# First laps of a fused attention and two-layer FFN kernel: a wider k product, weight conversions placed one to a lap, another order in the first lap

## The chip, the cores and the metric

The kernel runs on one NeuronCore of a Trainium2 chip. The metric is the device time of one execution in microseconds (us). Before the change the median of three runs is 961.79 us (961.52 to 962.55). About 0.2%, or 1.9 us, is the smallest difference that a comparison of this kernel can tell from none.

## The reference

Inputs are float32 except that the FFN weights come as float64 and stay so in DRAM; the kernel narrows them itself. Linear attention over 4 batches of 8 heads, 576 tokens, head size 64, is followed by two feed-forward layers on 2304 tokens of 512 features.

```python
def phi(x):
    proj = einsum('bhsd,df->bhsf', x, w_phi)               # 64 -> 128 features
    proj = proj - max(abs(proj), axis=-1, keepdims=True)
    return concatenate([exp(proj), exp(-proj)], axis=-1)
q_p, k_p = phi(q), phi(k)
kv  = einsum('bhsf,bhsd->bhfd', k_p, v);  z = sum(k_p, axis=2)
num = einsum('bhsf,bhfd->bhsd', q_p, kv)
den = einsum('bhsf,bhf->bhs', q_p, z)[..., None] + 1e-06
x   = (num / den), heads side by side                      # 2304 x 512
h   = x @ w_in;   x = max(0.01 h, h) @ w_out               # layer 1
h   = x @ w_in2;  out = (h * sigmoid(h)) @ w_out2          # layer 2
```

## The kernel before

Work on attention goes by pairs of heads, 16 pairs. Pairs 0 to 7 (`NFULL = 8`) are computed in full float32 in a first stage, the head; pairs 8 to 15 come later, in another form, between the matmuls of layer 1. Layer 1 goes over five tiles of about 460 tokens; for each tile it walks 16 blocks of 128 hidden features, with `emit_h(t, c)` (first product) and `emit_y(t, c)` (second). Layer 2 follows with a Strassen-like scheme.

The FFN weights must be converted from float64 before use. One conversion of a 128x512 block has a load into a tile of a ring of three (`raw`, L549), two ScalarE instructions (`ca`, L557 and L558), four VectorE instructions (`cd`, L564 to L567), a ScalarE copy to the high half (`ch`, L646) and a VectorE subtraction for the low half (`cs`, L651, recorded as L143). The conversions listed in `CONV` (L513) run in the head; the others are given to `prep` (L657) through `TODO` (L908) ahead of the blocks of the first tile.

One pair of the head takes these steps: load (`flq`, `flv`); k product on TensorE (`fpk` L290, and `fkt` for the last 64 tokens); row maximum and subtraction on VectorE (`fkd0..2`, L171 and L172); two exponentials on ScalarE (`fke`); q product (`fpq`) and its copy from PSUM on ScalarE (`fpc`, L339 and L341); the maximum over partitions on GpSimd (`fpr`, L350); its subtraction on VectorE (`fms`, L358); exponentials (`fqx`, L368 and L369); k times v on TensorE (`fkv`, L261 and L266); its copy on ScalarE (`fkc`, L378); numerator and denominator on TensorE (`fn0`, `fn1`, L391 and L395); the division on VectorE (`fnd`, L407 to L409); transposition (`fnt`) and the split into the x tiles (`ffx`, L287 and L143). A name like `fms1.0` means step `fms1` of pair 0.

The tiles `p`, `m` and `qh` have two buffers each, so the second half of one pair and the first half of the next share them in turn. PSUM banks come from a ring of eight (`bank`, L63).

The order is written out by hand. Each step of each pair has a due time: `LAP = 11.5` per pair plus an offset, with special offsets for pairs 0 to 2 in `FIRST` (L489). Each conversion has a lap and an offset kind in `LAPS` (L514). All steps are sorted by due time, and in the head `in_order` (L72) binds TensorE, ScalarE and VectorE to exactly that order. DMA issues and GpSimd are not bound. Steps due after `T0`, and everything of the FFN layers, are ordered by the planner of the framework.

```python
    for n, (lap, late) in enumerate(LAPS):
        for n_, o in (dict(cl=-14.0, ca=3.15, ...), dict(cl=-9.0, ca=1.4, ...))[late].items():
            seq.append((BASE + LAP * lap + o, n, n_))
```

So before the change laps 1, 3 and 5 hold two conversions each and laps 2 and 4 one: eight in all.

Of the kernel before, what the change touches and what calls it, by code (L numbers as in the profile page):

```python
# [19 lines left out]
def tile_linear_attention_ffn_ffn(ctx: ExitStack, tc: tile.TileContext, q, k, v, w_phi, w_in1, w_out1, w_in2, w_out2, out):  # L20


    nc = tc.nc
    B, H, S, D = 4, 8, 576, 64
    F = (w_phi.shape[1] - 128) // 3
# [9 lines left out]
    NFULL = 8  # L35
# [16 lines left out]
    def at(shape, dt, tag):  # L52
        return att_pool[0].tile(shape, dt, tag=tag, bufs=AB[0].get(tag, 1), name=tag)
# [4 lines left out]

    PRO = [True]

    ring = [0]

    def bank():  # L63

        if not PRO[0]:
            return ps("a")
        ring[0] += 1
        return ps("ay"[(ring[0] - 1) // 4 % 2])
# [16 lines left out]
    wc = at([128, 3 * F + 128], F32, "wc")  # L85
# [56 lines left out]
    def sub(out_, x, h):  # L142
        nc.vector.tensor_tensor(out_, x, h.bitcast(F32), op=ALU.subtract)  # L143

    def full(i):
        return i < NFULL
# [107 lines left out]
    def kv_sign(i, s):  # L254
        st = P[i]
        ke, va = st["ke"], st["va"]
        if s == 1:
            st["kv"] = bank()
        pv = st["kv"][:, 0 : 4 * NKV].rearrange("p (s j d) -> p s j d", s=2, j=2)
        vf = va.rearrange("p c d -> p (c d)")  # L260
        nc.tensor.matmul(pv[:, s, :, 0 : D + 1], ke[:, 8, s, :], va[:, 8:10], start=True, stop=False, skip_group_check=True)  # L261
        for j in range(2):
            for c in range(4):
                w = (4 * j + c) * (D + 1)
                g = 4 * j + c if full(i) else 2 * c + j
                nc.tensor.matmul(  # L266
                    pv[:, s, j], ke[:, g, s, :], vf[:, w : w + NKV], start=False, stop=(j == 1 and c == 3), skip_group_check=True
                )
        return pv

    def s_kv(i):
        st = P[i]
        for s in (1, 0):
            pv = kv_sign(i, s)
        h, l = st["KVH"], st["KVL"] = at([128, 2, 2, 2, D], F32R, "KVH"), at([128, 2, 2, 2, D], F32R, "KVL")
        for j in range(2):
            kv_, z_ = pv[:, :, j, 0:D], pv[:, :, j, D : D + 1].to_broadcast([128, 2, D])
            for slot, sr in ((j, kv_), (1 - j, z_)):
                nc.scalar.activation(h[:, j, :, slot, :], sr, AF.Copy)
                sub(l[:, j, :, slot, :], sr, h[:, j, :, slot, :])  # L280
# [9 lines left out]
    def f_pk(i):  # L290

        st = P[i]
        st["pk"] = [bank(), bank()]
        for c in range(4):
            for j in range(2):
                r = slice(64 * j, 64 * j + 64)
                o = st["pk"][j][:, c * F : (c + 1) * F]
                nc.tensor.matmul(o, st["kr"][r, c * 128 : (c + 1) * 128], wraw[r], start=True, stop=True)
# [159 lines left out]
    def s_fin(a):  # L458
# [13 lines left out]
    )  # L472
    head = dict(
        flq=load_qk, flv=load_v, fpk=f_pk, fkt=f_kt, fkv1=lambda i: kv_sign(i, 1), fkv0=lambda i: kv_sign(i, 0), fkc=f_kc,
        fkd0=f_kd(0), fkd1=f_kd(1), fkd2=f_kd(2), fke0=f_ke(0), fke1=f_ke(1),
    )
    for a in range(2):
        for n_, f in dict(fpq=f_pq, fpc=f_pc, fpr=f_pr, fms=f_ms, fqx=f_qx, fn=f_n, fnd=f_nd, fnt=f_nt, ffx=f_fx).items():
# [4 lines left out]
        flq=-8.0, fpq0=5.1, fpq1=5.11, fpk=6.2, fkt=7.2, fpc0=5.6, fpc1=6.2, fpr0=10.55,  # L483
# [4 lines left out]
    KEYS = {n_: o + LAP * lag for lag, d in enumerate((AHEAD, NEXT, HERE, PAST)) for n_, o in d.items()}  # L488
    FIRST = {  # L489
        0: dict(flq=-9.0, flv=-8.9, fpk=-5.0, fkt=-4.0, fpq0=-3.5, fpq1=-3.4, fpc0=-2.7, fpr0=-2.6, fke0=-2.0, fpc1=-1.0, fpr1=-0.9, fkd0=-3.4, fkd1=-2.2, fkd2=-1.0,  # L490
                fke1=-0.2, fms0=0.1, fqx0=1.7, fms1=3.3, fqx1=4.0, fn0=5.0, fn1=6.9, fnd0=7.0, fnd1=9.2),
        1: dict(flq=-8.8, flv=-8.0, fpk=-2.0, fkt=-1.0, fpq0=-0.6, fpq1=-0.5, fpc0=1.0, fpc1=2.8, fpr0=2.9, fms0=5.3, fqx0=7.0, fpr1=4.1, fms1=8.0),
        2: dict(flq=-8.5, fpq0=9.1, fpq1=9.11, fpk=10.2, fkt=11.2, fpc0=9.7, fpc1=10.3),
    }
    BASE = 8.9
# [14 lines left out]
    seq = [(T0 + LATER[i][n_] if n_ in LATER.get(i, ()) else t, i, n_) for t, i, n_ in seq]  # L510
    TL = T0 + 21.15 - min(OFF1.values())
    seq += [(TL + W * (i - NFULL) + o, i, n_) for i in range(NFULL, B * HP) for n_, o in OFF1.items()]
    CONV = [("wi", 0), ("wi", 1), ("wi", 2), ("wi", 3), ("wo", 0), ("wi", 4), ("wo", 1), ("wi", 5)]  # L513
    LAPS = [(1, 0), (1, 1), (2, 0), (3, 0), (3, 1), (4, 0), (5, 0), (5, 1)]  # L514
    for n, (lap, late) in enumerate(LAPS):
        for n_, o in (dict(cl=-14.0, ca=3.15, cd=6.1, ch=8.3, cs=10.1), dict(cl=-9.0, ca=1.4, cd=8.0, ch=8.8, cs=10.7))[late].items():
            seq.append((BASE + LAP * lap + o, n, n_))
    seq.sort()
    seq.reverse()
# [25 lines left out]
    wi, wo = {}, {}  # L545
# [39 lines left out]
    def load_wi(layer, c):  # L585
        w = (w_in1, w_in2)[layer].bitcast(U32)
        return load64(w[c].rearrange("p (f t) -> p f t", t=2))

    def load_wo64(w, c):
        return load64(w.bitcast(U32)[c * 128 : (c + 1) * 128, :].rearrange("p (f t) -> p f t", t=2))  # L590
# [28 lines left out]

    C = [dict() for _ in CONV]  # L620

    def c_load(n):

        kind, c = CONV[n]
        C[n]["raw"] = load_wi(0, c) if kind == "wi" else load_wo64(w_out1, c)
# [9 lines left out]
    def halves(kind, c):  # L635

        if kind == "wi":
            wi[0, c] = [wp.tile([128, KD, 128], F32R, tag=g, bufs=NC, name=g) for g in ("wih", "wil")]
            return [x.rearrange("p k f -> p (k f)") for x in wi[0, c]]
        wo[c] = wp.tile([128, 2, DM], F32R, tag="wo1", bufs=WOB, name="wo1")  # L640
        return wo[c][:, 0], wo[c][:, 1]

    def c_high(n):

        C[n]["h"] = halves(*CONV[n])
        nc.scalar.activation(C[n]["h"][0], C[n]["f"], AF.Copy)  # L646

    def c_low(n):

        kind, c = CONV[n]  # L650
        sub(C[n]["h"][1], C[n]["f"], C[n]["h"][0])  # L651
# [5 lines left out]
    def prep(kind, c):  # L657

        if (kind, c) in CONV:
            return  # L660
        raw = load_wi(0, c) if kind == "wi" else load_wo64(w_out1, c)
        f = narrow64(raw)
        split(f, *halves(kind, c))
        if kind == "wo":
            nc.sync.dma_start(wos[c], wo[c].bitcast(F32))
# [239 lines left out]
    split_consts()  # L905
    run_att(T0)
    PRO[0] = False
    TODO = [("wi", 6), ("wi", 7)], [("wo", 2), ("wi", 8)], [("wi", 9), ("wi", 10)], [("wo", 3), ("wi", 11)], [("wo", 4), ("wi", 12), ("wi", 13)], [("wo", 5), ("wi", 14)], [("wo", 6), ("wi", 15)]  # L908

    def jobs_of(m, p):  # L910
        for _ in prep_w7(m, p):
# [20 lines left out]
    for s, (t, c) in enumerate((t, c) for t in range(len(tiles1)) for c in range(NC)):  # L932
        if t:
            wo[c] = load_wo(c)
        else:
            for x in TODO[c] if c < len(TODO) else [("wo", c)]:
                prep(*x)
# [120 lines left out]
```

## Time and profile before

| | |
|---|---|
| median of three runs | 961.79 us |
| profiled execution, its own time | 963.05 us |
| its span | 961.3 us |
| PE busy (matmul) | 940.5 us, 98% |
| PEld busy (weight loads) | 886.3 us, 92% |
| DVE busy | 646.9 us, 67% |
| ACT busy | 596.8 us, 62% |
| POOL busy | 70.0 us, 7% |
| mean granted TensorE clock | 0.994 |

The profile is of one execution. PE is TensorE, DVE is VectorE, ACT is ScalarE, POOL is GpSimd, SP issues DMAs. Idle time of an engine is set down with what ended it. A float32 matmul is recorded as two instructions. Matmuls are pipelined and their ends are modelled, so that the start of one to the start of the next is the better measure of pace.

### The profile page before, as it was taken

What the parts mean: (1) busy time and instruction counts of PE and PEld (TensorE: products, weight loads), DVE (VectorE), ACT (ScalarE), POOL (GpSimd) and SP (SyncE); (2) the same over time, 40 slices, a digit from 0 to 9 for tenths busy, and PEclk for the clock granted to TensorE, in tenths of its full rate; (3) what the DMA queues carried; (4) which work ended last, traced back from release to release, by engine and by line L of the source; (5) the groups of instructions that cost most, each with busy time, mean ns of one, the idle gap of its engine ahead of it and who ended that gap; (6) DMA issues with size and microseconds to landing.
All of it is one profiled execution on the core that took longest, in us unless ns stands there. A gap on an engine that the chain in (4) does not pass through costs nothing.

```text
span 961.3 us, 15911 instructions
## 1 busy us (share of the span) xinstructions
PE 940.5 (98%) x5446; PEld 886.3 (92%) x5446; DVE 646.9 (67%) x1280; ACT 596.8 (62%) x1224; POOL 70.0 (7%) x38
## 2 busy tenths in 40 slices
PE   7999999999999999999999999999999999999998
PEld 6888888898999988988888999999999999999998
DVE  5899989865666655288778767777762595624853
ACT  5788877676777766466555655665554565544553
POOL 3333000211111111000000000000000000000000
PEclk9999899999999999999999999999999999999999
DMA  6443489644333332399999999896988878886884
GB/s 248 142 139 111 158 250 326 226 142 119 119 109 119 93 121 69 114 360 380 359 331 326 377 352 342 306 341 237 301 290 294 244 233 273 293 286 216 250 279 136
DMA packets 102529, 226.15 MB, mean 235 GB/s; under 512 B 15024, under 2 KB 25264, under 8 KB 102448
## 3 DMA queue, kind: packets, MB, share of 16 engines
q1 hardware_dynamic: 102160, 224.86, 70.0%
q8 instruction: 44, 0.72, 0.3%
q14 instruction: 37, 0.30, 0.1%
q10 hardware_dynamic: 288, 0.26, 0.1%
HBM read 177.82 MB, written 47.22 MB: 234 GB/s over the span
## 4 chain that ended last, share of the span: by engine, by line
PE 74%; DMA 9%; DVE 9%; ACT 5%; issue 2%; SPq 1%; POOL 0%; DVEq 0%; ACTq 0%
PE ps_y L868 18%; PE ps_y L732 15%; PE ps_a L712 14%; PE ps_a L792 10%; PE ps_y L792 8%; PE ps_a L266 3%; DMA d<-rec 2%; DMA rec<-e 2%; PE ps_a L443 1%; DVE t L566 1%; PE ps_y L391 1%; DMA qr<-in_q_dram 1%; DMA raw<-in_moe_w_in_dram 1%; PE ps_a L391 1%; DVE km L171 1%
## 5 line engine op out<-in xcount | busy, mean ns | idle before, releaser
L868 PE MATMUL ps_y<-gt,ws 128*128 128x384 f32 x1008 | 177.2, 336 | 0.0
L868 PEld LDWEIGHTS ps_y<-gt,ws 128*128 128x128 f32 x1008 | 176.5, 188 | 0.0
L732 PE MATMUL ps_y<-gh,wo 128*128 128x460 f32 (+1 forms) x640 | 150.4, 373 | 2.5 <-ACT gh L575 2.5
L732 PEld LDWEIGHTS ps_y<-gh,wo 128*128 128x128 f32 x640 | 119.0, 188 | 15.9 <-ACT gh L575 3.1
L712 PE MATMUL ps_a<-xh,wih 128*128 128x460 f32 (+1 forms) x320 | 119.5, 374 | 0.4 <-ACT g L715 0.3
L712 PE MATMUL ps_a<-xl,wih 128*128 128x460 f32 (+1 forms) x320 | 118.9, 371 | 0.0
L712 PE MATMUL ps_a<-xh,wil 128*128 128x460 f32 (+1 forms) x320 | 118.8, 371 | 0.0
L792 PE MATMUL ps_a<-xs,ws 128*128 128x384 f32 x546 | 104.7, 338 | 1.6 <-DMA ws<-w7s 1.6
L792 PEld LDWEIGHTS ps_a<-xs,ws 128*128 128x128 f32 x546 | 96.7, 188 | 2.3 <-ACT xs L575 1.9
L575 ACT ACTIVATE gt<-g 128x384 fp32r<-128x384 f32 x120 | 62.8, 524 | 52.8 <-PE ps_y L868 50.9
L143 DVE TENSOR_TENSOR gt<-g,gt 128x384 fp32r<-128x384 f32 x120 | 66.5, 556 | 35.9 <-ACT gt L575 35.5
L792 PE MATMUL ps_y<-xs,ws 128*128 128x384 f32 x462 | 88.5, 338 | 0.2 <-DVE g L768 0.2
L732 PE MATMUL ps_y<-gl,wo 128*128 128x460 f32 (+1 forms) x320 | 82.7, 373 | 0.0
L792 PEld LDWEIGHTS ps_y<-xs,ws 128*128 128x128 f32 x462 | 81.7, 188 | 0.6 <-DVE g L768 0.5
L143 DVE TENSOR_TENSOR gl<-g,gh 128x460 fp32r<-128x460 f32 (+1 forms) x80 | 50.9, 637 | 33.8 <-ACT gh L575 28.8
L715 ACT ACTIVATE g<-ps_a 128x460 f32<-128x460 f32 (+1 forms) x80 | 44.0, 551 | 38.9 <-PE ps_a L712 38.3
L712 PEld LDWEIGHTS ps_a<-xh,wih 128*128 128x128 f32 x320 | 60.1, 188 | 7.3 <-DVE ke L172 0.5
L732 PEld LDWEIGHTS ps_y<-gl,wo 128*128 128x128 f32 x320 | 60.1, 188 | 6.8
L712 PEld LDWEIGHTS ps_a<-xh,wil 128*128 128x128 f32 x320 | 60.1, 188 | 6.8
L712 PEld LDWEIGHTS ps_a<-xl,wih 128*128 128x128 f32 x320 | 60.3, 188 | 6.1
L231 POOL PARTITION_ALL_REDUCE m<-p x16 | 34.8, 2178 | 242.6 <-ACT p L229 203.7
L575 ACT ACTIVATE gh<-g 128x460 fp32r<-128x460 f32 (+1 forms) x80 | 46.7, 585 | 8.4 <-PE ps_y L732 7.4
(164 smaller groups left out, 1593.0 us busy)
## 6 DMA issues: line engine op xcount, KB each, us to landing
ws<-w7s SPq DMA_DIRECT2D x336, 256.0 KB, 3.7
wo<-wos SPq DMA_DIRECT2D x64, 512.0 KB, 4.8
w7s<-wst SPq DMA_DIRECT2D x48, 512.0 KB, 5.7
raw<-in_moe_w_in_dram SPq DMA_DIRECT2D x32, 512.0 KB, 5.1
raw<-in_moe_w_out_dram SPq DMA_DIRECT2D x32, 512.0 KB, 5.1
wos<-wo SPq DMA_DIRECT2D x16, 512.0 KB, 4.0
va<-in_v_dram SPq DMA_DIRECT2D x16, 325.0 KB, 3.4
qr<-in_q_dram SPq DMA_DIRECT2D x16, 288.0 KB, 4.2
```

The source lines that it names most:

```text
L143: nc.vector.tensor_tensor(out_, x, h.bitcast(F32), op=ALU.subtract)
L171: nc.vector.tensor_reduce(km[:, 0:ng], src, op=ALU.max, axis=AX.X, apply_absolute_value=True)
L231: nc.gpsimd.partition_all_reduce(m, p, 128, bass_isa.ReduceOp.absmax)
L266: nc.tensor.matmul(pv[:, s, j], ke[:, g, s, :], vf[:, w : w + NKV], start=False, stop=(j == 1 and c == 3), skip_group_check=True)
L391: nc.tensor.matmul(pb[:, w : w + NNUM], e[:, s, cs], KV[:, s, j], start=(s == 0), stop=(s == 1))
L443: nc.tensor.matmul(o, lhs, st[m, a][:, s, j * w : (j + 1) * w], start=(n == 0), stop=(n == 5))
L575: nc.scalar.activation(h, f, AF.Copy)
L712: nc.tensor.matmul(ph, a[:, kk, :], b_[:, kk, :], start=(m == 0), stop=(m == 3 * KD - 1))
L715: nc.scalar.activation(g, ph, AF.Prelu, alpha=0.01)
L732: nc.tensor.matmul(Y[t][d][:, 0:n], a[:, ds_], b_, start=(c == 0 and m == 0), stop=(c == NC - 1 and m == 1), skip_group_check=True)
L792: nc.tensor.matmul(bank[b_], w[:, a, kk], x[:, c, kk], start=(first and m == 0), stop=(m == 5), skip_group_check=True)
L868: nc.tensor.matmul(bank[b_][db], w[:, a, db], t[:, c], start=(first and p == 0 and m == 0), stop=(p == NP - 1 and m == 2), skip_group_chec ...
```

## The change

`fpk` of pairs 0 and 1 multiplies 128 rows by the block-diagonal weight `wc[:, 0:2F]` (256 columns, four matmuls) in place of eight matmuls of 64 rows by 128 columns. `kv_sign` reads the groups of those pairs in the matching order. In the first lap `fms1.0`, `fqx1.0` and `fkc.0` come earlier, as do `fpr0.1`, `fms0.1`, `fpr1.1` and `fms1.1`. Conversions: one in lap 0 (offset kind 2), one in lap 1 (kind 3, written as lap 0 with offsets a lap larger), one in each of laps 2, 3 and 4, two in lap 5: seven. The eighth, `("wi", 5)`, goes to the front of `TODO`.

```diff
-    ring = [0]
+    ring, WIDE = [0], 2
@@ kv_sign
-                g = 4 * j + c if full(i) else 2 * c + j
+                g = 4 * j + c if WIDE <= i < NFULL else 2 * c + j
@@ f_pk
         for c in range(4):
+            if i < WIDE:
+                o = st["pk"][c // 2][:, (c % 2) * 2 * F : (c % 2 + 1) * 2 * F]
+                nc.tensor.matmul(o, st["kr"][:, c * 128 : (c + 1) * 128], wc[:, 0 : 2 * F], start=True, stop=True)
+                continue
             for j in range(2):
@@ FIRST
-                fke1=-0.2, fms0=0.1, fqx0=1.7, fms1=3.3, fqx1=4.0, fn0=5.0, fn1=6.9, fnd0=7.0, fnd1=9.2),
-        1: dict(flq=-8.8, flv=-8.0, fpk=-2.0, fkt=-1.0, fpq0=-0.6, fpq1=-0.5, fpc0=1.0, fpc1=2.8, fpr0=2.9, fms0=5.3, fqx0=7.0, fpr1=4.1, fms1=8.0),
+                fke1=-0.2, fms0=0.1, fqx0=1.7, fms1=1.5, fqx1=2.6, fkc=2.7, fn0=5.0, fn1=6.9, fnd0=7.0, fnd1=9.2),
+        1: dict(flq=-8.8, flv=-8.0, fpk=-2.0, fkt=-1.0, fpq0=-0.6, fpq1=-0.5, fpc0=1.0, fpc1=2.8, fpr0=1.1, fms0=4.2, fqx0=7.0, fpr1=3.0, fms1=6.0),
@@ conversions
-    CONV = [("wi", 0), ("wi", 1), ("wi", 2), ("wi", 3), ("wo", 0), ("wi", 4), ("wo", 1), ("wi", 5)]
-    LAPS = [(1, 0), (1, 1), (2, 0), (3, 0), (3, 1), (4, 0), (5, 0), (5, 1)]
+    CONV = [("wi", 0), ("wi", 1), ("wi", 2), ("wi", 3), ("wo", 0), ("wi", 4), ("wo", 1)]
+    LAPS = [(0, 2), (0, 3), (2, 0), (3, 0), (4, 0), (5, 0), (5, 1)]
-        ... (dict(cl=-14.0, ca=3.15, cd=6.1, ch=8.3, cs=10.1), dict(cl=-9.0, ca=1.4, cd=8.0, ch=8.8, cs=10.7))[late]
+        ... (dict(cl=-14.0, ca=3.15, cd=6.1, ch=8.3, cs=10.1), dict(cl=-9.0, ca=1.4, cd=8.0, ch=8.8, cs=10.7), dict(cl=-7.9, ca=4.5, cd=4.6, ch=7.3, cs=15.2), dict(cl=-7.8, ca=14.65, cd=17.6, ch=19.8, cs=21.6))[late]
-    TODO = [("wi", 6), ("wi", 7)], [("wo", 2), ("wi", 8)], ...
+    TODO = [("wi", 5), ("wi", 6), ("wi", 7)], [("wo", 2), ("wi", 8)], ...
```

The order of the first lap on the three bound engines, read off the due times (steps that change place in bold):

- DVE before: fkd0.0 fkd1.0 fkd2.0 fms0.0 fkd0.1 fkd1.1 fkd2.1 fms1.0 fms0.1 fnd0.0 fms1.1 fnd1.0 fkd0.2
- DVE after: fkd0.0 fkd1.0 fkd2.0 fms0.0 fkd0.1 **fms1.0** fkd1.1 fkd2.1 fms0.1 **cd.0** **fms1.1** fnd0.0 fnd1.0 fkd0.2
- ACT before: fpc0.0 fke0.0 fpc1.0 fke1.0 fpc0.1 fqx0.0 fke0.1 fpc1.1 fqx1.0 fkc.0 fke1.1 fqx0.1 fpc0.2
- ACT after: fpc0.0 fke0.0 fpc1.0 fke1.0 fpc0.1 fqx0.0 fke0.1 **fqx1.0 fkc.0 fpc1.1 ca.0** fke1.1 fqx0.1 **ch.0** fpc0.2
- PE, both: fpk.0 fkt.0 fpq.0 fpk.1 fkt.1 fpq.1 fkv.0 fn0.0 fn1.0 fpq.2 fpk.2 fkt.2 fkv.1 fnt.0 fpq.3 fpk.3 fkt.3 fn.1 fkv.2 and so on

## Rows read from the trace of the kernel before

**Rows 1.** The page, busy tenths in 40 equal slices of the span, VectorE.
```profile
DVE  5899989865666655288778767777762595624853
```

**Rows 2.** Windows: stretch, length, then busy (count) of PE PEld DVE ACT POOL; clock, DMA, GB/s.
```profile
18.85:22.36 3.51, 3.51 (x18) 3.51 (x19) 0.00 (x0) 1.30 (x2) 1.89 (x1) 0.56 0.03 13
...
98.20:104.93 6.73, 6.73 (x37) 6.73 (x37) 6.73 (x18) 5.83 (x11) 0.00 (x0) 0.58 0.43 152
104.93:133.00 28.07, 27.25 (x174) 24.63 (x172) 25.34 (x58) 20.08 (x37) 0.00 (x0) 1.00 0.65 206
133.00:204.90 71.90, 70.26 (x362) 63.28 (x361) 60.43 (x114) 51.67 (x98) 7.03 (x3) 1.00 0.74 249
204.90:961.30 756.40, 747.99 (x4138) 712.27 (x4136) 475.93 (x929) 444.95 (x913) 27.82 (x13) 1.00 0.73 246
```

**Rows 3.** Waits of PE over the whole span: total us, times, longest.
```profile
PE ps_y L732 <- ACT gh L575: 2.5, 2, 2.3
...
PE ps_a L261 <- ACT ke L180: 1.6, 1, 1.6
```

**Rows 4.** Timeline of PE in the first lap: start us, us, instruction, [idle before <-releaser].
```profile
13.19 1.95 PE L266 MATMUL ps_y<-va,ke 128*128 128x128 f32 x16
18.85 3.52 PE L391 MATMUL ps_y<-KV,qh 128*128 128x128 f32 x16 [3.71 <-ACT KV L378]
...
25.60 1.06 PE L298 MATMUL ps_y<-wc,kr 64*128 64x128 f32 x16
...
26.91 0.39 PE L261 MATMUL ps_a<-va,ke 128*128 128x130 f32 x2
```

**Rows 5.** Timeline of PE: the end of `fn1` of pairs 0 to 4.
```profile
23.99 0.61 PE L395 MATMUL ps_a<-KV,qh 128*128 128x130 f32 x4
...
37.69 0.61 PE L395 MATMUL ps_a<-KV,qh 128*128 128x130 f32 x4
...
50.58 0.61 PE L395 MATMUL ps_y<-KV,qh 128*128 128x130 f32 x4
...
61.88 0.61 PE L395 MATMUL ps_a<-KV,qh 128*128 128x130 f32 x4
...
75.20 0.61 PE L395 MATMUL ps_y<-KV,qh 128*128 128x130 f32 x4
```

**Rows 6.** Timeline of DVE in the first lap.
```profile
9.82 1.95 DVE L358 TENSOR_TENSOR m<-p,m 128x512 f32<-128x512 f32 x1 [0.34 <-POOL m L350]
...
12.41 0.69 DVE L172 TENSOR_TENSOR ke<-ps_y,km 128x512 f32<-128x512 f32 x1
...
22.40 0.16 DVE L407 TENSOR_SCALAR d<-ps_y 128x4 f32<-128x4 f32 x1 [5.72 <-PE ps_y L391]
...
22.81 0.42 DVE L409 TENSOR_TENSOR x<-ps_y,d 128x256 f32<-128x256 f32 x1
```

**Rows 7.** Timeline of ACT in the first lap, and the start of a conversion.
```profile
16.17 0.38 ACT L339 ACTIVATE p<-ps_y 128x256 f32<-128x256 f32 x1 [1.43 <-DVE m L358]
...
16.92 0.76 ACT L368 ACTIVATE qh<-m 128x640 f32<-128x640 f32 x1
...
18.18 0.62 ACT L378 ACTIVATE KV<-ps_y 128x512 f32<-128x512 f32 x1
...
27.86 0.71 ACT L557 ACTIVATE t<-raw 128x512 f32<-128x512 f32 x1
```

**Rows 8.** Timeline of POOL: the second all-reduce of pair 0.
```profile
9.81 2.34 POOL L350 PARTITION_ALL_REDUCE m<-p  x1
```

**Rows 9.** Timeline of DVE: two conversions start in turn, and a low half.
```profile
33.48 0.42 DVE L564 TENSOR_SCALAR t<-t 128x512 f32<-128x512 f32 x1
...
35.73 0.42 DVE L564 TENSOR_SCALAR t<-t 128x512 f32<-128x512 f32 x1
...
49.85 0.69 DVE L143 TENSOR_TENSOR wil<-r,wih 128x512 fp32r<-128x512 f32 x1
```

**Rows 10.** The chain that ended last, in order of time, one piece: start, us, what.
```profile
133.52 5.48 DMA raw<-in_moe_w_in_dram
```

More of the change, by code (lines that the diff above doesn't have):

```diff
@@ L512, in tile_linear_attention_ffn_ffn @@
     seq += [(TL + W * (i - NFULL) + o, i, n_) for i in range(NFULL, B * HP) for n_, o in OFF1.items()]
-    CONV = [("wi", 0), ("wi", 1), ("wi", 2), ("wi", 3), ("wo", 0), ("wi", 4), ("wo", 1), ("wi", 5)]
-    LAPS = [(1, 0), (1, 1), (2, 0), (3, 0), (3, 1), (4, 0), (5, 0), (5, 1)]
+    CONV = [("wi", 0), ("wi", 1), ("wi", 2), ("wi", 3), ("wo", 0), ("wi", 4), ("wo", 1)]
+    LAPS = [(0, 2), (0, 3), (2, 0), (3, 0), (4, 0), (5, 0), (5, 1)]
     for n, (lap, late) in enumerate(LAPS):
-        for n_, o in (dict(cl=-14.0, ca=3.15, cd=6.1, ch=8.3, cs=10.1), dict(cl=-9.0, ca=1.4, cd=8.0, ch=8.8, cs=10.7))[late].items():
+        for n_, o in (dict(cl=-14.0, ca=3.15, cd=6.1, ch=8.3, cs=10.1), dict(cl=-9.0, ca=1.4, cd=8.0, ch=8.8, cs=10.7), dict(cl=-7.9, ca=4.5, cd=4.6, ch=7.3, cs=15.2), dict(cl=-7.8, ca=14.65, cd=17.6, ch=19.8, cs=21.6))[late].items():
             seq.append((BASE + LAP * lap + o, n, n_))
@@ L907, in tile_linear_attention_ffn_ffn @@
     PRO[0] = False
-    TODO = [("wi", 6), ("wi", 7)], [("wo", 2), ("wi", 8)], [("wi", 9), ("wi", 10)], [("wo", 3), ("wi", 11)], [("wo", 4), ("wi", 12), ("wi", 13)], [("wo", 5), ("wi", 14)], [("wo", 6), ("wi", 15)]
+    TODO = [("wi", 5), ("wi", 6), ("wi", 7)], [("wo", 2), ("wi", 8)], [("wi", 9), ("wi", 10)], [("wo", 3), ("wi", 11)], [("wo", 4), ("wi", 12), ("wi", 13)], [("wo", 5), ("wi", 14)], [("wo", 6), ("wi", 15)]
     def jobs_of(m, p):
```

## Prediction

> **What bounds the kernel now.** I read the page's slices first: TensorE shows nines almost throughout, and VectorE shows eights and nines only from the second slice to about the eighth, that is up to some 190 us, and sixes and sevens after that [rows 1]. So the changed stage lies where two engines are near full. The windows split it. From 204.90 on PE is busy for 747.99 of 756.40 us at full clock [rows 2]: whatever time is won earlier is simply carried to the end, since nothing there waits for a date. From 104.93 to 204.90 PE is busy for 97.5 of 100 us, and DVE for 85.8 [rows 2]: PE sets the pace there, but DVE is close behind, and PE's 1.6 us wait for `ke` of pair 8 [rows 3] shows that DVE's and ACT's backlog does end one thing last there. Before that, in the head, the timeline of PE shows the laps. The ends of `fn1` lie at 23.99, 37.69, 50.58, 61.88 and 75.20 [rows 5], so the laps take 13.70, 12.89, 11.30 and 13.32 us. The reader sees a pattern: 11.30 is PE's own lap, without a stall, and the longer ones follow the laps that hold two conversions, in which DVE is late. In lap 0, PE stands still for 3.71 us before `fn0.0` because ACT copies KV late, and the 16 matmuls behind that gap take 3.52 us where 16 of the same shape before it took 1.95 [rows 4]; the granted clock of that stretch is 0.56, the mean of a part at 1.2 GHz and a part at 2.4 [rows 2].
>
> **Lap 0.** Before, ACT was through with `fke0.1` at 14.74 (16.17 less its wait of 1.43), waited for DVE to free the `p` buffer, copied `fpc1.1` for 0.75 (16.92 less 16.17), did `fqx1.0` in 1.26 and reached KV at 18.18 [rows 7]. After, `fms1.0` stands right behind `fkd0.1` on DVE, which ends at 13.10 (12.41 + 0.69) [rows 6]; POOL's maximum is there at 12.15 (9.81 + 2.34) [rows 8]. At some 0.8 us it is done at 13.9, before ACT wants it. So ACT does `fqx1.0` from 14.74 to 16.0 and can copy KV then, if `fkv.0` is through. That ended at 15.14 (13.19 + 1.95) [rows 4].
>
> The wide product moves it. Its cost is not in the trace. From below: 16 instructions of the old form take 1.06 us [rows 4]; if the wide form, eight instructions, cost the same, nothing is added. From above: the same columns streamed through the whole array, 16 times 128, took 1.95 [rows 4], 0.9 more. I take 0.9, since that row streams just these columns at full clock. For pair 0 it costs nothing, since PE waits for q behind it anyway (without that cover, 0.9); for pair 1 it puts the end of `fkv.0` at 16.04, level with ACT's 16.0. KV is thus copied at 16.05, 2.1 earlier than 18.18, and `fn0.0` starts at about 16.7 in place of 18.85. PE's gap shrinks from 3.71 to about 0.7.
>
> The two halves of `fn` then take full-clock time: 3.5 us in place of 5.1 (18.85 to 23.99). The last four matmuls start at 20.3, not 23.99: 3.7 earlier. What is late next is DVE, since the conversion now stands ahead of the divisions. ACT: KV to 16.5, `fpc1.1` 0.75, two `ca` instructions of 0.71 that overlap, some 1.2 [rows 7], so `ca.0` ends at 18.45. DVE: `cd.0` 2.25 (35.73 less 33.48) [rows 9] to 20.7, `fms1.1` 0.7, `fnd0.0` 0.83 (22.40 to 23.23) [rows 6] and `fnd1.0`, half as wide again, 0.9: 23.1. `fkv.1` needs the bank that `fnd1.0` frees. PE itself had 2.92 us from `fn1.0`'s last matmuls to `fkv.1` (23.99 to 26.91) [rows 4, 5], which leads to 23.2: the two come together, and `fkv.1` starts at 23.2, not 26.91. **Lap 0 gives 3.7 us.** Its bounds: 4.2, if the steps ahead of `fms0.0` win half a microsecond too, because the wide product of pair 0 no longer waits for the second half of the weights; and a loss of 1.8, if KV comes no earlier and both wide products lie on the path at 0.9 each.
>
> The other moved steps of pair 1 (`fpr0.1`, `fpr1.1`, `fms0.1`, `fms1.1`) only follow the new order of DVE and ACT, and POOL has no other work. On SP the two raw loads of the first laps keep their place behind `flv.1`, so no load of a pair moves.
>
> On DVE, `fms0.0` took 1.95 us when it started with the all-reduce (9.82 against 9.81) [rows 6, 8], about 1.2 longer than a free one, and ended before POOL did (11.77 against 12.15). `cd.0` meets the all-reduce of `fpr1.1`, which runs from 17.3 to 19.6; its instructions with two SBUF inputs start near 19.2, past such a 1.2 us hold, so I cost this at nothing. The Trainium skill, SBUF — State Buffer, "Who interferes with whom", says that a DVE instruction with two SBUF inputs is blocked until a GpSimd instruction that reads SBUF has wholly finished. The trace disagrees on "wholly". By that rule `cd.0` would stand until 19.6 and the forecast would be some 0.5 us slower.
>
> **Laps 1 to 4.** Lap 1 was held on PE by nothing (26.91 to 37.69 is one run), so it keeps its length and the next marker falls at 34.0. Its second conversion cost the time after it: 12.89 where a lap of PE takes 11.30, a gain of 1.6. The same in lap 3: 13.32 becomes 11.30, a gain of 2.0. That one conversion fits into 11.30 is what the lap ending at 61.88 shows [rows 5]; if it does not fit four times in a row, DVE sets a lap between 11.30 and 13.32, and at worst both terms are gone. Markers: 45.3, 56.6, 67.9. **Head: 3.7 + 1.6 + 2.0 = 7.3 us earlier.** Lap 5 has two conversions before and after, and starts from PE's wait in both, so its shape should be kept.
>
> **The eighth conversion.** `wi5` now runs after the head: DVE 2.25 + 0.6 (0.69, overlapping) [rows 9], 2.9 in all, and ACT some 1.7. Its load stands ahead on SP's queue in the place that `wi6`'s had, and each later load one place later. Lower bound 0: PE is nearly gapless from 104.93 to 204.90, wi5 is read only by the sixth block of the first tile, and DVE has 2.7 us free up to 133.00 and 11.5 behind it [rows 2]. Upper bound 2.9: PE's wait for `ke` [rows 3] hangs on DVE's and ACT's order, behind the conversions, and there PE would arrive 7.3 earlier while DVE comes only 4.4 earlier. I take two thirds, 1.9, nearer to the bound since that wait exists already and the free time on DVE is partly DMA latency (a raw load took 5.48 us to land [rows 10]).
>
> **Sum.** -7.3 + 1.9 = -5.4 us. The profiled execution took 963.05 us (span 961.3), so 957.6 by its own clock; the median of the runs stands 1.26 lower, at 961.79, which gives 956.4.
>
> **Rivals.**
> - *The head's end runs better too* (chance 0.20). Behind PE's wait of 2.3 us for `gh` [rows 3], PE runs 6.73 us at clock 0.58 [rows 2]. If the planner's new order closes that gap, 6.73 x 0.42 = 2.8 us are won, and `wi5` is hidden: -10.1, 951.7. For it: PE's work is all there. Against: the order there is the planner's, and it gets more conversion work, not less.
> - *`wi5` is paid at the head's end* (0.17). If its 2.9 us push KV of pair 6 on ACT, PE's gap before `fn0.6` grows by as much, on top of the 1.9: -2.5, 959.3. For it: DVE has no idle time from 98.20 to 104.93 [rows 2].
> - *Lap 0 gives nothing* (0.12): KV is not copied earlier, since ACT or DVE waits for POOL in the new order, and the change does not do what it says. -3.6 + 1.9 = -1.7, 960.1, no difference that can be told.
> - *Slower* (0.07). The three raw tiles are a ring and SP issues in order. If `wi5`'s load costs the ring one more exposed turn in front of pair 8's loads, the price is 5.48 for the landing, some 1.2 on ACT and 1.5 on DVE until the tile is free, 8.2, and 2.9 for the conversion: -7.3 + 11.1 = +3.8, 965.6. It decides from the point at which pair 8's k and q land later than before. Against it: `wi5` comes at the very front, long before those loads.
>
> **Numbers.** The forecast has 0.44, with a range of its own of 954.0 to 958.4 (`wi5` free and lap 0 at 4.2 on one side, all of `wi5` paid and lap 0 a microsecond short on the other). Faster by over 0.2% (1.9 us, what a measurement of this kernel can tell) holds it and the first two rivals: 0.81. Within: 0.12. Slower: 0.07. To hold 8 in 10, the range reaches down to most of the first rival and up past the second: 951.7 to 960.0.
>
> **What would show it.** PE's gap before the first L391 falls under 1 us and the 16 matmuls behind it take about 1.95; L395 starts near 20.3, 34.0, 45.3, 56.6 and 67.9; `cd.0` fills DVE's gap of 5.72 before `fnd0.0`; the laps 1 to 4 are all near 11.3. The wait for `ke` of pair 8 grows from 1.6 to about 3.5. Wrong would be: the low clock still granted near 20 us (lap 0 gave nothing), laps above 12 us with one conversion (DVE or ACT is the bound, not PE), or markers as forecast with no gain at 204.90 (the conversions bound the first tile).

## The result and the profile after

The changed kernel takes 951.19 us (median of 4 runs, 950.29 to 953.87) beside 961.65 us for the kernel before on the same chip: a ratio of 0.9899 (0.9873 to 0.9925), some 10 us in place of the 5.4 of the forecast. By the ratio the 961.79 of before become 952.1, at the low end of the range of 951.7 to 960.0. The profiled execution took 950.29 us (span 948.5, clock 0.996). The profiled execution of before lay 1.4 us above its median, that of after 0.9 below; so the spans differ by 12.8, the medians by 10.5. One of the fourteen executions of the changed kernel in this document took 2382.55 us, with its matmuls about twice as long (those of L872 678 ns for 336), VectorE's busy time as ever and no cause found; it is in no number below.

Line numbers are four higher than before behind the k product (L391 is L395, L395 is L399, L564 is L568, L732 is L736). The markers first, the timeline of PE at the last matmuls of each pair's `fn1`, pairs 0 to 7:

```profile
20.74 0.61 PE L399 MATMUL ps_a<-KV,qh 128*128 128x130 f32 x4
...
35.22 0.61 PE L399 MATMUL ps_a<-KV,qh 128*128 128x130 f32 x4
...
46.52 0.61 PE L399 MATMUL ps_y<-KV,qh 128*128 128x130 f32 x4
...
57.82 0.61 PE L399 MATMUL ps_a<-KV,qh 128*128 128x130 f32 x4
...
69.12 0.61 PE L399 MATMUL ps_y<-KV,qh 128*128 128x130 f32 x4
...
80.40 0.61 PE L399 MATMUL ps_a<-KV,qh 128*128 128x130 f32 x4
...
98.57 0.61 PE L399 MATMUL ps_a<-KV,qh 128*128 128x130 f32 x4
...
122.45 0.61 PE L399 MATMUL ps_a<-KV,qh 128*128 128x130 f32 x4
```

Against [rows 5] they come 3.25, 2.47, 4.06, 4.06 and 6.08 earlier (forecast 3.7, 3.7, 5.3, 5.3, 7.3). Laps 2 to 5 take 11.30, 11.30, 11.30 and 11.28: the long laps are gone. Before, the markers of pairs 5 and 7 were here:

```profile
86.50 0.61 PE L395 MATMUL ps_a<-KV,qh 128*128 128x130 f32 x4
...
128.42 0.61 PE L395 MATMUL ps_a<-KV,qh 128*128 128x130 f32 x4
```

So the head hands on 6.0 us at pair 7.

The rest of the gain comes later. VectorE copies a finished tile of layer 1 out of PSUM; the starts of the first copy of the first and of the fifth tile, before and then after:

```profile
204.95 1.18 DVE L737 COPY o<-ps_y 128x462 f32<-128x462 f32 x2
...
610.01 1.18 DVE L737 COPY o<-ps_y 128x460 f32<-128x460 f32 x2 [0.68 <-PE ps_y L732]
```

```profile
197.25 1.19 DVE L741 COPY o<-ps_y 128x462 f32<-128x462 f32 x2 [0.47 <-PE ps_y L736]
...
598.09 1.18 DVE L741 COPY o<-ps_y 128x460 f32<-128x460 f32 x2 [0.68 <-PE ps_y L736]
```

The lead is 7.7 us at the first tile, 11.9 at the fifth, 12.8 at the end of the span. The windows say what went. They are those of [rows 2]; the columns are the same:

```profile
18.85:22.36 3.51, 3.51 (x32) 3.19 (x32) 3.30 (x5) 2.55 (x6) 1.55 (x1) 1.00 0.04 14
98.20:104.93 6.73, 6.73 (x52) 6.47 (x52) 6.05 (x14) 5.72 (x12) 0.00 (x0) 1.00 0.48 161
104.93:133.00 28.07, 27.25 (x159) 24.25 (x158) 25.20 (x57) 19.16 (x38) 0.00 (x0) 1.00 0.68 221
133.00:204.90 71.90, 71.90 (x381) 65.26 (x380) 62.68 (x117) 55.59 (x105) 6.42 (x3) 1.00 0.75 258
204.90:948.50 743.60, 739.10 (x4089) 705.06 (x4088) 469.62 (x920) 439.25 (x902) 27.82 (x13) 1.00 0.74 248
```

This stretch of the first lap now runs at full clock (1.00 where it was 0.56). From 133 to 204.90 PE is busy for all of 71.90 us; before it stood still for 1.64, the wait for `ke` of pair 8 in [rows 3]. Behind 204.90 its idle time is 4.50 us, where it was 8.41. The wait that was to grow to 3.5 us is gone, and no step of pair 8 was edited.

The first lap on PE:

```profile
3.89 2.85 PE L297 MATMUL ps_a<-wc,kr 128*128 128x256 f32 x8
...
17.06 2.05 PE L395 MATMUL ps_y<-KV,qh 128*128 128x128 f32 x16 [0.98 <-ACT KV L382]
...
24.12 0.39 PE L261 MATMUL ps_a<-va,ke 128*128 128x130 f32 x2
```

The gap before `fn0.0` is 0.98 where [rows 4] had 3.71, and the 16 matmuls take 2.05 in place of 3.52. On ACT, DVE and POOL in the same lap:

```profile
16.43 0.58 ACT L382 ACTIVATE KV<-ps_y 128x512 f32<-128x512 f32 x1
```

```profile
10.35 1.95 DVE L362 TENSOR_TENSOR m<-p,m 128x512 f32<-128x512 f32 x1 [0.85 <-POOL m L354]
...
18.39 1.20 DVE L568 TENSOR_SCALAR t<-t 128x512 f32<-128x512 f32 x1 [1.38 <-ACT t L561]
19.62 1.06 DVE L569 TENSOR_SCALAR t<-t 128x512 uint32<-128x512 uint32 x1
20.71 0.70 DVE L570 SCALAR_TENSOR_TENSOR t<-raw,t 128x512 uint32<-128x512 uint32 x1
21.55 0.69 DVE L571 CUSTOM_DVE_ANT_0 r<-t,r 128x1024 uint16<-128x1024 uint16 x1
```

```profile
17.88 2.52 POOL L354 PARTITION_ALL_REDUCE m<-p  x1 [1.72 <-ACT p L345]
```

Two things fall short here. `fms0.0` starts at 10.35 where [rows 6] had 9.82. The wide product of pair 0 stands ahead of q and takes 2.85 us, where that of pair 1 takes about 2.0; why is not shown, since the trace has no reading of the clock before 5.8 us. And the four instructions of `cd.0` take 3.85 us from 18.39 to 22.24, against 2.25 in [rows 9]; the first two, 0.42 each when free, take 1.20 and 1.06 beside the all-reduce.

At the head's end nothing moved but the dates. PE still waits twice and runs the 32 matmuls slowly:

```profile
90.53 0.68 PE L736 MATMUL ps_y<-gh,wo 128*128 128x462 f32 x2 [2.29 <-ACT gh L579]
92.10 6.63 PE L395 MATMUL ps_a<-KV,qh 128*128 128x128 f32 x32 [0.88 <-ACT KV L382]
```

### The profile page after: what moved, and what is told of

It reads as the page before. It is cut to its first block, busy times and chain, and to the rows that moved or that the text cites. A ratio compares the mean times of both kernels' runs of the same rounds, so it can differ in the third digit from the quotient of the medians.

```text
span 948.5 us, 15879 instructions
## 1 busy us (share of the span) xinstructions
PE 937.0 (99%) x5430; PEld 885.9 (93%) x5430; DVE 646.7 (68%) x1280; ACT 597.7 (63%) x1224; POOL 69.6 (7%) x38
## 4 chain that ended last, share of the span: by engine, by line
PE 95%; DVE 3%; ACT 1%; DMA 1%; issue 0%; POOL 0%; ACTq 0%
PE ps_a L716 21%; PE ps_y L736 21%; PE ps_y L872 19%; PE ps_a L796 10%; PE ps_y L796 8%; PE ps_a L266 4%; PE ps_a L447 3%; PE ps_a L395 2%; PE ps_y L395 1%; PE ps_y L266 1%; DMA ws<-w7s 1%; PE ps_a L261 1%; PE ps_a L227 0%; PE ps_a L226 0%; PE ps_a L332 0%; PE ps_a L194 0%
## 5 line engine op out<-in xcount | busy, mean ns | idle before, releaser
L872 PE MATMUL ps_y<-gt,ws 128*128 128x384 f32 x1008 | 177.2, 336 | 0.0
L872 PEld LDWEIGHTS ps_y<-gt,ws 128*128 128x128 f32 x1008 | 176.5, 188 | 0.0
L736 PE MATMUL ps_y<-gh,wo 128*128 128x460 f32 (+1 forms) x640 | 149.5, 372 | 2.3 <-ACT gh L579 2.3
L736 PEld LDWEIGHTS ps_y<-gh,wo 128*128 128x128 f32 x640 | 119.4, 188 | 15.4 <-ACT gh L579 2.4
L736 PE MATMUL ps_y<-gl,wo 128*128 128x460 f32 (+1 forms) x320 | 82.8, 374 | 0.0
L736 PEld LDWEIGHTS ps_y<-gl,wo 128*128 128x128 f32 x320 | 59.9, 188 | 7.0 <-DVE gl L143 0.3
```

What stands on the lines that cost most here:

```text
L736: nc.tensor.matmul(Y[t][d][:, 0:n], a[:, ds_], b_, start=(c == 0 and m == 0), stop=(c == NC - 1 and m == 1), skip_group_check=True)
L872: nc.tensor.matmul(bank[b_][db], w[:, a, db], t[:, c], start=(first and p == 0 and m == 0), stop=(p == NP - 1 and m == 2), skip_group_chec ...
```

## The experiments

Three theories stand in the expectations. **S**: the steps of the change carry the gain, lap by lap. **P**: any edit of the head makes the planner redraw the order of the work behind it, and that order is worth microseconds of its own. **B**: the gain behind the head grows with the lead that the head hands on. "Rest" is the span less pair 7's marker. Marker 6 is the sixth marker (pair 5). Markers and rest are read from one execution of each kernel; medians and ratios rest on several.

| kernel | median us (runs) | ratio to before, interval | marker 6 | pair 7 | rest |
|---|---|---|---|---|---|
| before | 961.65 (4) | | 86.50 | 128.42 | 832.9 |
| after | 951.19 (4) | 0.9899 (0.9873, 0.9925) | 80.40 | 122.45 | 826.1 |
| e1 wide product alone | 960.1 (10) | 0.9982 (0.9963, 1.0001) | 87.62 | 128.23 | 831.7 |
| e2 all but the wide product | 952.49 (4) | 0.9905 (0.9868, 0.9941) | 79.95 | 122.12 | 827.6 |
| e3 first lap's order alone | 956.03 (7) | 0.9939 (0.9917, 0.9962) | 83.13 | 123.96 | 829.3 |
| e4 conversions alone | 956.65 (8) | 0.9948 (0.9928, 0.9968) | 83.03 | 123.57 | 829.5 |
| e5 eight in the head | 955.51 (10) | 0.9944 (0.9926, 0.9963) | 82.93 | 123.82 | 831.2 |
| e6 `wi5` a block later | 952.6 (4) | 0.9908 (0.9881, 0.9935) | 80.55 | 122.60 | 827.8 |
| e8 `cd.0` behind the divisions | 953.96 (4) | 0.9924 (0.99, 0.9947) | 82.31 | 124.03 | 827.4 |
| e9 e5, PE's order of after | 955.12 (6) | 0.9926 (0.9909, 0.9944) | 82.86 | 124.65 | 829.7 |
| e10 after, PE's order of e5 | 959.15 (12) | 0.9966 (0.9951, 0.9981) | 80.48 | 122.33 | 834.5 |
| after, again | 951.51 (3) | 0.9887 (0.9853, 0.992) | | | |
| after, repeated | 952.78 (6) | 0.9897 (0.9878, 0.9915) | 80.83 | 121.48 | 827.6 |
| e11 e5, every order of after | 949.82 (6) | 0.9876 (0.9848, 0.9905) | 83.01 | 121.30 | 829.0 |

Medians of before beside them were 961.4 to 962.6, its single runs 957.4 to 966.4; a difference of one microsecond between two rows is not resolved. From marker 6 to pair 7's marker the kernels take 41.7 to 42.2 us, or 40.5 to 40.9, or 38.3 (e11). The windows give that stretch a granted clock of 0.92 in before and after, of 0.96 in the repeat of after, e3 and e5, and of 1.00 in e11. So pair 7's marker carries over a microsecond that differs between two executions of one kernel: 42.05 and 40.65 in after.

**The parts alone.** e1 is the changed kernel with the due times and conversions of before; e2 has the narrow product; e3 is before with the new `FIRST`; e4 is before with the seven conversions (its `TODO` is that of the change).

```diff
 e2
-    ring, WIDE = [0], 2
+    ring, WIDE = [0], 0
 e3, against before
-                fke1=-0.2, fms0=0.1, fqx0=1.7, fms1=3.3, fqx1=4.0, fn0=5.0, ...
+                fke1=-0.2, fms0=0.1, fqx0=1.7, fms1=1.5, fqx1=2.6, fkc=2.7, fn0=5.0, ...
-        1: dict(..., fpr0=2.9, fms0=5.3, fqx0=7.0, fpr1=4.1, fms1=8.0),
+        1: dict(..., fpr0=1.1, fms0=4.2, fqx0=7.0, fpr1=3.0, fms1=6.0),
 e4, against before
-    LAPS = [(1, 0), (1, 1), (2, 0), (3, 0), (3, 1), (4, 0), (5, 0), (5, 1)]
+    LAPS = [(0, 2), (0, 3), (2, 0), (3, 0), (4, 0), (5, 0), (5, 1)]
```

> The kernel before with the wide k product of pairs 0 and 1 and nothing else. Three theories. S (steps): the time is what the markers of the head say, carried to the end. P (planner): what is gained behind the head comes from the order that the planner of the framework draws for the rest, which any edit redraws, so it has no fixed sign and does not follow the head's markers. B (backlog): what is gained behind the head comes from arriving earlier with the conversions further ahead, so it grows with the head's gain and is zero without one. Here: the wide product of pair 0 runs at the low clock and puts the first maximum about 0.5 us later, that of pair 1 adds 0.8 on PE ahead of a KV copy that is late anyway. Markers (the last four matmuls of fn1 of pairs 0 to 4): 24.0 to 24.5, 38.2, 51.1, 62.4, 75.7. S: +0.5 us, 962.2. B: the same. P: anywhere within 4 us of 962.2.

> The changed kernel with the old k product (64 rows) for pairs 0 and 1 too. The first maximum comes 0.5 us earlier than in the changed kernel, the end of fkv.0 about 1.3 earlier. First marker 20.2 in place of 20.74; fkv.1 still hangs on cd.0, which hangs on ca.0, all 0.5 earlier; markers 20.2, 34.7, 46.0, 57.3, 68.6. S and B: 0.5 us below the changed kernel, about 950.7. P: within 4 us of that, either side.

> The kernel before with the new order of the first lap alone: old k product, eight conversions in their old laps. KV of pair 0 is copied near 15.6 and PE's gap before fn0.0 falls from 3.7 to about 0.8, at full clock; no conversion stands before the divisions. First marker 19.9, then with two conversions in laps 1 and 3 as before: 33.4, 46.3, 57.6, 70.9, that is 4.3 earlier at the last. S: 957.4. B: gains behind the head in proportion, so about 954.5. P: 957.4 give or take 4.

> The kernel before with the new places of the conversions alone: seven in the head, one a lap, wi5 behind it; old k product, old order of the first lap. PE's gap of 3.7 us before fn0.0 and the low clock stay, and cd.0 lies in DVE's gap. Markers 24.0, 37.7, 49.0, 60.3, 71.6: 3.6 earlier at the last. S: 958.0. B: about 955.6. P: 958.0 give or take 4. If wi5 costs what the forecast put on it, 1.9 more in each.

Measured: in the head the parts act as S says. The order alone closes PE's gap (1.30 us) and gives 3.4 at marker 6; the conversions alone leave the gap at 3.57 and give 3.5, all laps from lap 2 on being 11.3; the wide product alone costs 1.1, though its time is not longer (0.9982). The sum, 5.7, is near the 6.1 of the whole. In the whole change the wide product costs 0.45 by one profile each: the first marker of e2 is at 20.29, of after at 20.74 (20.82 to 21.35 in the other profiles of this first lap), and the medians can't tell them apart.

But S does not cover the time of the whole change. By the ratios after gains 9.7 us, and 9.9 repeated, against leads of 6.0 and 6.9 at pair 7's marker. e2, e6 and e8 too gain 2.8 to 3.0 us more than their lead there; e1, e3 and e4 gain 0.2 to 1.5 more. Each of these numbers is uncertain by some 2 us. So e3 and e4 by themselves do not show a gain behind the head: their rests are some 3.5 us shorter than that of before, but the profiles of e3 and e4 are of executions 1.0 and 1.8 us below the median, that of before of one 1.4 us above.

**Where the eighth conversion goes.** e5 keeps the new first lap and the wide product and runs all eight conversions in the head; e6 does `wi5` one block later.

```diff
 e5
-    LAPS = [(0, 2), (0, 3), (2, 0), (3, 0), (4, 0), (5, 0), (5, 1)]
+    LAPS = [(0, 2), (0, 3), (2, 0), (3, 0), (3, 1), (4, 0), (5, 0), (5, 1)]
-    TODO = [("wi", 5), ("wi", 6), ("wi", 7)], [("wo", 2), ("wi", 8)], ...
+    TODO = [("wi", 6), ("wi", 7)], [("wo", 2), ("wi", 8)], ...
 e6
-    TODO = [("wi", 5), ("wi", 6), ("wi", 7)], [("wo", 2), ("wi", 8)], ...
+    TODO = [("wi", 6), ("wi", 7)], [("wo", 2), ("wi", 8), ("wi", 5)], ...
```

> The changed kernel with wi5 back in the head, as the second conversion of lap 3 where the kernel before had one: eight in the head, two in laps 3 and 5. Markers to the fourth as in the changed kernel (20.7, 35.2, 46.5, 57.8), then 2.0 later: 71.1, 82.4. S with wi5 free behind the head: +2.0, 953.2. With the 1.9 that the forecast put on wi5 behind the head: 951.3, no difference. P: 953.2 give or take 4.

> The changed kernel with wi5 as the third conversion of the second block of the first tile in place of the first of the first block; nothing else differs, and the order of the head up to its end is the same. Markers as in the changed kernel to 80.4. S and B: the same time within 1 us, 951.2; B in particular: no wait of PE behind 133 us, since the head's lead is the same. P: the rest is drawn anew, waits of 1 to 5 us turn up, 952 to 956.

e5 was the turn. It hands on 4.6 us at pair 7 and has less conversion work left behind the head than after, and its rest is 831.2, close to that of before; by the ratio it gains only 0.8 more than its lead. That speaks against B. The order of the instructions in the traces, engine by engine, gives P its form: behind the head the kernels differ only up to about 222 us, within the first tile of layer 1 and just behind it. After, e2, e6 and e8 have one and the same order on PE there; before and e5 share another, on ScalarE and VectorE too; e1, e3 and e4 have each their own. In one profile each, the rests go by these families: 826.1 to 827.8 (with the repeat of after), 831.2 to 832.9, and 829.3 to 831.7. e5 has the wait of before again, a little longer (timeline of PE):

```profile
189.03 0.49 PE L261 MATMUL ps_a<-va,ke 128*128 128x130 f32 x2 [2.05 <-ACT ke L180]
```

e6 moves nothing that can be told from after: whether `wi5` stands in the first block or the second is free. For P as put it was a miss: no order is drawn anew on PE, and no wait of 1 to 5 us turns up behind the head.

**`cd.0` away from the all-reduce.** e8 puts the first conversion's VectorE part behind the divisions of pair 0.

```diff
-        dict(cl=-7.9, ca=4.5, cd=4.6, ch=7.3, cs=15.2)
+        dict(cl=-7.9, ca=4.5, cd=9.3, ch=11.4, cs=15.2)
```

> The changed kernel with cd.0 behind the two divisions of pair 0 on VectorE in place of ahead of fms1.1, and ch.0 later to match. In the changed kernel the first two instructions of cd.0 took 1.20 and 1.06 us against 0.42 and 0.43, while POOL's all-reduce ran. If that collision and its place ahead of the divisions hold fkv.1 back: fms1.1 at 20.4 with POOL's end, divisions done near 22.3, fkv.1 near 23.6 in place of 24.12 (PE's own pace), cd.0's instructions back at 0.42 and 0.43, markers 20.7, 34.7, 46.0, 57.3, 68.6, time 950.7 (S). If PE's pace alone sets fkv.1, nothing moves: 951.2.

It met the next all-reduce. The timelines of e8, DVE and then POOL:

```profile
23.41 0.42 DVE L568 TENSOR_SCALAR t<-t 128x512 f32<-128x512 f32 x1
23.86 1.27 DVE L569 TENSOR_SCALAR t<-t 128x512 uint32<-128x512 uint32 x1
```

```profile
23.41 2.40 POOL L354 PARTITION_ALL_REDUCE m<-p  x1 [2.61 <-ACT p L343]
```

Lap 1, from the first marker to the second, took 15.78 us against 14.48 in after. The median is 2.4 us above that of after beside it on the same chip (953.96 against 951.51), with intervals that overlap. The instruction that starts together with the reduce, at 23.41, takes its free 0.42; the next, begun inside it, takes 1.27. In after both begin inside the reduce and both are held; in e4, whose `cd.0` meets that reduce too, they take 0.71 and 1.06. So the offset of the change was the better of two bad places; one clear of both reduces was not tried.

**The changed kernel again**, to see how far two profiles of one kernel differ.

> The changed kernel once more, on one chip with the experiments beside it. Its profile showed no wait of PE between 133 and 450 us where that of before had 4.7 us of them. If these waits belong to the order of the instructions (P), this profile shows the same: markers within 0.1 us of 20.74, 35.22, 46.52, 57.82, 69.12, 80.40, 98.57, and under 0.3 us of idle PE from 133 to 450; the time is 951.2 within 1. If they differ from one execution of a kernel to the next, 1 to 3 us of idle time turn up there and the time of the profiled execution moves with them.

> The changed kernel once more, for a second profile and as the neighbour of the two others. All theories: 951 us, pair 7's marker at 122.4, the rest at 826 to 826.5 if the profiled times repeat within half a microsecond.

The first gave 951.51 us and no profile to set beside the others. The second agrees with the first profile of after to 0.43 us at marker 6 and to 0.1 at the first tile's copy (197.16), but not between and behind them: pair 7's marker comes 0.97 earlier, and the rest is 1.5 us longer, where half a microsecond was expected. From 133 to 450 us PE is idle for 1.2 us in it, against 0.1 in the first profile and 4.8 in before. So the wait for `ke` is gone in both, but about a microsecond of such waits belongs to the single execution.

**The order by itself.** e5 and after issue the same matmul instructions (5,430 records in either trace). Their orders differ in 210 of the places from the 608th to the 979th instruction, all in the first tile and just behind it. Edges without a wait can bind one kernel to the other's order, with no step changed. e9 gives e5 the PE order of after; e10 gives after the PE order of e5; e11 gives e5 the order of after on PE, DVE and ACT, which also makes SP's the same.

```diff
+    ORDER = dict(PE=[...], DVE=[...], Activation=[...])
+    nosync = mybir.DependencyInfo(mybir.DependencyClass.NoSync, mybir.DependencyReason.DATA)
+    for e, order in ORDER.items():
+        ins = [x for x in nc.cur_bb.bb.instructions if x.engine == getattr(mybir.EngineType, e) and len(x.outs)]
...
+        line = [ins[j] for a, b in order for j in range(a, b + 1)]
+        for x, y in zip(line, line[1:]):
+            tc.add_manual_dep(y, x.name, nosync, reason="order")
```

> The kernel with eight conversions inside the head (955.5 us, rest of 831.2 us behind pair 7's marker), with one thing added: edges that make TensorE's instructions behind the head stand in the order that the changed kernel has (126 rows of the first tile of layer 1; no instruction is added or removed; VectorE and ScalarE are still ordered by the planner). P (the planner's order of the first tile decides): the marker of pair 7 stays at 123.8, PE's wait for ke of pair 8 (2.05 us) and the waits behind it go, the rest falls from 831.2 to 826 to 828, the time to 951 to 952.5. B and S (the rest follows the head's lead, or the conversions): nothing changes, 955.5. If VectorE's and ScalarE's order is what matters, not TensorE's: 955 or above, with new waits on PE.

> The changed kernel with one thing added: edges that make TensorE's instructions behind the head stand in the order of the kernel with eight conversions in the head, which is also the order of the kernel before. All steps of the change are kept. P: markers as in the changed kernel (122.45 for pair 7), PE waits for ke of pair 8 by 1.5 us or more, the rest grows from 826.05 to about 830 to 831, the time from 951.2 to 955 to 956. B and S: nothing changes, 951.2.

> The kernel with eight conversions inside the head (955.5 us, pair 7's marker at 123.8 to 124.7, rest of 829.7 to 831.2) with edges that give TensorE, VectorE and ScalarE, and through them SyncE, the very order behind the head that the changed kernel has. It differs from the changed kernel only in that the eighth conversion stands in the head, and from the kernel with eight only in the order behind it. P (the order of all engines together decides): marker at 123.8 or a little later, no wait of PE over 1 us between 133 and 200, a rest of 826 to 828, 951.5 to 953. If it was the conversions' place or the head's lead after all (S, B): 955 to 956, with the rest at 830 or more.

e10 keeps the whole head of after and loses 6.4 us of the 9.8 that after gains beside it on the same chip (959.15 against 952.78; the intervals lie apart). With the lead of after it gains nothing behind the head, which refutes B. The wait is back (timeline of PE, e10):

```profile
189.13 0.49 PE L261 MATMUL ps_a<-va,ke 128*128 128x130 f32 x2 [2.54 <-ACT ke L180]
```

Behind it the granted clock is 0.54 from 189.6 to 193.3 us. The first tile's copy starts at 202.57, 80.2 us behind pair 7's marker, where after has 74.8 (its repeat 75.7) and e5, with its own ScalarE and VectorE order, 77.0. So the 6.4 us look like the price of a TensorE order which the other engines don't follow, more than before's own order costs.

e9 was a miss for P as put. With PE's order alone the wait for `ke` goes, a wait for `gh` takes its place (timeline of PE, e9), and the time stays (955.12 for 955.51):

```profile
189.75 1.10 PE L736 MATMUL ps_y<-gh,wo 128*128 128x462 f32 x4 [2.00 <-ACT gh L579]
```

e11, with all engines in the order of after, is 5.7 us faster than e5 (949.82 for 955.51; the intervals lie apart): the order decides, but of all engines together. It came out by another way than expected, though. Its first tile takes 75.0 us from pair 7's marker, 2.0 less than e5's, as P said. The first copies of that tile, e11 and then e5:

```profile
196.32 1.19 DVE L741 COPY o<-ps_y 128x462 f32<-128x462 f32 x2 [0.47 <-PE ps_y L736]
```

```profile
200.86 1.19 DVE L741 COPY o<-ps_y 128x462 f32<-128x462 f32 x2
```

The other 2.6 were won ahead of it, between the markers of pairs 5 and 6 (14.43 us for 17.01), where the edges changed what the planner still had free: there ScalarE and VectorE stand in an order that neither after nor e5 has. Timeline of PE there, e11 and then e5:

```profile
93.35 0.69 PE L736 MATMUL ps_y<-gh,wo 128*128 128x462 f32 x2 [2.47 <-ACT gh L579]
93.88 3.73 PE L395 MATMUL ps_a<-KV,qh 128*128 128x128 f32 x32
```

```profile
94.64 5.47 PE L395 MATMUL ps_a<-KV,qh 128*128 128x128 f32 x32 [0.87 <-ACT KV L382]
```

In e11 ScalarE copies KV of pair 6 before it does `gh`:

```profile
91.82 0.59 ACT L382 ACTIVATE KV<-ps_y 128x512 f32<-128x512 f32 x1
...
92.69 0.61 ACT L579 ACTIVATE gh<-g 128x462 fp32r<-128x462 f32 x1
```

PE then stands still once and not twice, and the granted clock from 83 to 104 us is 1.00. In after, from 82 to 103, it is 0.84. The rest of e11, 829.0, is above the 828 expected; the excess lies behind the first tile (754.0 us from the copy to the end, e5 754.1, after 751.3, its repeat 752.0), in this one profile. e11 has the lowest median of all, but is not told apart from after by the intervals of the ratios.

## Why the prediction came out as it did

**The first step that failed: that a lead is simply carried on.** "Whatever time is won earlier is simply carried to the end" took the work behind the head as fixed. It was not: the planner drew it anew. The profiles put 6.0 us of the 12.8 in the head, 1.7 between pair 7's marker and the first copy (the vanished wait for `ke`, 1.64; in the repeat's profile that stretch gives 0.9), and 5.1 behind it. Of the 12.8, 2.3 are only the distance of the two profiled executions from their medians. What the order is worth by itself e11 shows: with no step changed it is 5.7 us faster than e5, in the profiles 2.0 of it in the first tile, and 2.6 at the head's end by an order that after does not have. e5 and after lie 4.0 us apart on one chip (955.51 against 951.51), but 1.4 of that stand at pair 7's marker already. So some 2 us in the first tile are shown to be the order's. How the rest of the gain behind the head splits into the order's after-effects, DMA arrival (PE's wait for `ws` shrank from 1.6 to 0.8) and the scatter of single executions is open; the same kernel's two profiles differ there by 0.7, and e11 shows that the order of the first tile alone does not fix it.

**The eighth conversion, a term mis-sized: 1.9 forecast, nothing measured.** The bound taken was PE's wait for `ke`, which was to grow. It vanished, and e6 shows that `wi5` can stand elsewhere for the same time. The stretches with and without it agree too. From marker 6 to pair 7's marker, where it now runs, after takes 42.05 us and before 41.92 at a granted clock of 0.92, the repeat of after 40.65 and e5 40.89 at 0.96; the first tile takes 74.8 and 75.7 in after, and 75.0 in e11, which has the same order there. The argument that PE arrives earlier at a fixed `ke` was wrong because neither place was fixed.

**Lap 0, a term mis-sized: 3.7 forecast, 2.5 measured at the second marker.** KV was copied at 16.43, not 16.05; the gap closed and the clock stayed up, as forecast. Missing are 0.45 at the first marker, which goes with the wide product, priced at nothing for pair 0 (e2, without it, has that marker at 20.29, where 20.3 was forecast; one profile each, and e3, also without it, has 20.63). Missing are also 0.78 in lap 1, which was to keep its 13.70 and took 14.48. e3, which has no conversion in lap 0, keeps 13.70 exactly; so the 0.78 comes with `cd.0`, whose meeting with the all-reduce I had also priced at nothing. Where `cd.0` falls into DVE's gap, in e4, the lap stays at 13.70 although it is held there too. On PE, 0.41 of it is a wait of `fkt.2`, here with the end of `fnd0.0` on DVE:

```profile
23.82 0.46 PE L308 MATMUL ps_y<-wc,kt 128*128 128x128 f32 x2 [0.41 <-PE ps_y L302]
```

```profile
23.30 0.42 DVE L413 TENSOR_TENSOR x<-ps_y,d 128x256 f32<-128x256 f32 x1
```

The profile names PE itself as the releaser, but `fkt.2` starts 0.10 us behind the end of that division in e2 and e5 too. By an estimate from these rows, without the 1.6 us that `cd.0` took too long the division would have ended near 22.1, before PE was ready at 23.41. `fkv.1`, which the forecast had wait for `fnd1.0`, started at 24.12, ahead of that one's end at 24.81.

I had assumed that only instructions with two SBUF inputs are held and that those come late enough. The trace shows the hold on `cd.0`'s first two, which have one input. The Trainium skill, SBUF — State Buffer, "Who interferes with whom", says that `tensor_scalar` can run in a mode that uses both ports and then contends with GpSimd; the trace agrees (1.20 and 1.06 us for 0.42). The rule that I set aside there gave 0.5, nearer to the 0.78 than my nothing, but for the instructions with two inputs, and those began behind the all-reduce (20.71 against 20.40).

**The second conversions of laps 1 and 3: 1.6 and 2.0, as forecast.** 12.89 became 11.30 and 13.32 became 11.30; e4 shows the same with nothing else changed. One conversion fits into a lap of PE three times in a row. Lap 5 kept its shape. One of the signs of being wrong did come, a lap above 12 us with one conversion: lap 1, at 14.48. The prediction contradicts itself there, since it wants laps 1 to 4 near 11.3 while its markers leave lap 1 at 13.70. Its reading of [rows 1] passes over eights and a nine behind the eighth slice; nothing hangs on that.

**The rivals.** The time is that of "the head's end runs better too" (951.7), but its mechanism did not happen in after: the 32 matmuls still took 6.63 us. It did happen in e11, for 2.6 against e5, about the forecast 2.8. "`wi5` paid at the head's end", "lap 0 gives nothing" and "slower" are refuted by the markers. So the sum was 5.4, and the right one was 6.0 for the head, nothing for `wi5`, and some 4 behind the head that no step named, some 2 of them shown to be the order's. That the range held the time is in part luck: its low end was put there for a rival that did not happen.

## What to carry to other kernels

Where a planner orders work behind the part that is edited, compare the instruction order of both programs before putting a gain down to the edit, and leave room in the range for an order drawn anew: here it was as large as the steps. To test it, bind one version to the other's order with edges that wait for nothing, on all engines, since one engine's order alone can cost more than either. And TensorE's two short waits in a row can cost nearly as much in clock as in standing still: behind waits of 2.3 and 0.9 us, 6.63 us for matmuls that take 3.73 at full clock.

## What was not expected of the hardware

- In-place TENSOR_SCALAR of 128x512 with one SBUF input took 0.71 to 1.27 us when it began inside a GpSimd all-reduce of 2.4 to 2.5 us (after, e4, e8), and 0.42 when it began with it or away from it.
- The 32 matmuls behind the same two waits (2.3 and 0.9 us) took 6.63 us in one execution of the changed kernel and 5.21 in the other, with a granted clock of 0.81 and 0.90 from marker 6 to the next; behind a single wait of 2.47 us (e11) they took 3.73. Behind a single wait of 2.54 us in e10 the granted clock was 0.54 from 189.6 to 193.3 us.
- The wide product of pair 0 took 2.85 us for eight instructions at the start of the kernel; for pair 1 about 2.0.
